# Clearing and first evictions on ScalarE, two-tile norms and a later Q projection in the head of a two-layer attention and MLP kernel

## The chip, the cores and the metric

The kernel runs on one core of a Trainium2 chip. The metric is the device time of one execution in microseconds (us), as the median of several runs. The core has five engines with a queue of instructions each: TensorE (PE in the profile), VectorE (DVE), ScalarE (ACT), GpSimd (POOL) and SyncE (SP, which here only issues DMAs).

## The reference

Two layers run one after the other over the same 2048 tokens of width 512. Each has an attention with 32 query heads of size 16 that share one K and one V, and then a mixer with an MLP:

```python
def _A_ref(x, wq, wk, wv, wo):          # H = 32, Dh = 16
    q = (x @ wq).reshape(B, S, H, Dh).transpose(0, 2, 1, 3)
    k = x @ wk
    v = x @ wv
    p = softmax(einsum("bhqd,bkd->bhqk", q, k) * Dh ** -0.5)
    o = einsum("bhqk,bkd->bhqd", p, v)
    return o.transpose(0, 2, 1, 3).reshape(B, S, H * Dh) @ wo

def _B_ref(x, w1, w2, w3, w4):
    h = gelu(layernorm(x) @ w1)
    hs = concatenate([g0, g1, g2, g3], -1) @ w2   # quarters of h, moved by +1, -1, +2, -2 tokens
    x1 = x + hs
    return x1 + gelu(layernorm(x1) @ w3) @ w4

x = x + _A_ref(layernorm(x), ...);  x = x + _B_ref(layernorm(x), ...)   # layer 0
x = x + _A_ref(layernorm(x), ...);  x = x + _B_ref(layernorm(x), ...)   # layer 1, same weights
```

## The kernel before

**A planner writes the order.** Every piece of work is declared with `op(engine, emit, reads, writes, dur, prio)`. `Plan.run` is a list scheduler: it keeps a modelled clock for each engine and, whenever one is free, takes the ready operation with the lowest `prio` number. The result is a fixed order for each engine, which the hardware then follows in order, with semaphores between engines. A change of one early operation therefore can re-order everything declared later. The length of an operation in the plan is `dur`; `port=True` keeps those GpSimd and VectorE operations apart that share a memory port in the plan.

**Attention.** The 2048 queries of a layer are cut into chunks of 512 (the last two of layer 1 have 256), and each chunk into 8 blocks of 4 heads. A block meets 16 tiles of 128 keys, and each tile in two halves of two heads. In all there are 2048 halves of 128x1024 scores. A half takes one of two ways. In the first, TensorE makes the scores (`qk`, L1011) and ScalarE takes the exponential into `EA` (L1055), with two slots in PSUM so that two halves are under way. In the second, VectorE makes an approximate exponential with integer arithmetic (`J`, L1076), and GpSimd or VectorE add two shifted copies (`JK`, L1086); the program calls such a half a pair. The method `assign` gives a half to the second way when VectorE has time and its inputs are there. TensorE then multiplies with V (L1134): from `VP` for the first way, from `VD`, three scaled copies of V, for the second. The sum of a block is kept in one PSUM bank, `ACC`.

**Layer passage.** In the first chunk of layer 1 the keys of layer 1 are not all there yet. The blocks therefore run over the first 6 tiles of keys, then up to 11, then the rest. At the end of the first two passes VectorE spills `ACC` to memory (L1152) or adds to what was spilled (L1146), fourteen times in all. Meanwhile the MLP of the last chunk of layer 0 is finished and K of layer 1 is made from it (`next_kv`, `ln_in`, `kv`, L868).

**Between scores.** Gelus run on ScalarE (L1385, L1465). They need a table load, and another one before the next exponential. Where TensorE would be idle, `filler` inserts matmuls of zeros (`PB<-ONES,NIL`, L631) to keep it busy.

**The head** (`head`, L665) is what the change touches. `load_x` (L672) fetches x in eight loads of two tiles. GpSimd clears `VD` and `QT` (`fill`, L684), since K and Q lie there in slices with zeros between. Then for each of the four chunks of four tiles: `ln_in` takes statistics (L743), a reciprocal root by GpSimd's power (L763, its input made at L765), the normalised rows (`apply`, L780), and eight or sixteen transposes on TensorE (L798) with VectorE's copies to `YT` (L805). In layer 0 the four tiles of a chunk go through each step together; in layer 1 they go in portions of two, through `across` (L825, L830). `kv` makes K (L868, evicted at L875) and V (L883, evicted at L888 and L893). `qproj` makes Q: with `direct=True` block by block with its zeros (L940, evicted at L947), else in pairs of blocks (L631, evicted to `QS` at L922) which SP's DMAs spread to `QT` (L928).

In the head the lines that set the order of Q are:

```python
        for c in range(4):
            tiles = list(range(4 * c, 4 * c + 4))
            self.ln_in(0, tiles, prio=-6 + 0.5 * c)
            self.kv(0, tiles, prio=-6 + 0.5 * c)
            if c == 0:
                self.qproj(0, 0, prio=-6, blocks=(0, 1), direct=True)
            if c == 2:
                self.qproj(0, 0, prio=-5, blocks=range(2, 8))
```

So blocks 0 and 1 of the first chunk come straight after its K and V, and blocks 2 to 7 after K and V of the third chunk.

Of the kernel before, what the change touches and what calls it, by code (L numbers as in the profile page):

```python
# [485 lines left out]
def t_ps(n):  # L486
    return 0.066 + n * 1.043e-3
# [6 lines left out]
def t_x2(n):  # L494
    return 0.066 + n * 0.522e-3
# [14 lines left out]
class Kernel:  # L510
# [154 lines left out]
    def head(self):  # L665
# [40 lines left out]
        vd = [("VD", i, t) for i in range(2) for t in range(16)]  # L706
        fill("POOL", self.VD, 0.0, vd, 2.8, -7)
        for j in range(3):
            fill("POOL", self.VD[:, j, :, :, 16:17], self.PARTS[j], vd, 0.2, -7)
        fill("POOL", self.QT[:, 0, 2:8, :], 0.0, [("QT", 0, b) for b in range(2, 8)], 2.7, -7)  # L710
        fill("POOL", self.QT[:, 1, :, :], 0.0, [("QT", 1, b) for b in range(8)], 3.6, 2)
        for c in range(4):
            tiles = list(range(4 * c, 4 * c + 4))
            self.ln_in(0, tiles, prio=-6 + 0.5 * c)
            self.kv(0, tiles, prio=-6 + 0.5 * c)
            if c == 0:
                self.qproj(0, 0, prio=-6, blocks=(0, 1), direct=True)
            if c == 2:
                self.qproj(0, 0, prio=-5, blocks=range(2, 8))
        fill("POOL", self.SELC, 0.0, [("SELC",)], 0.1, 3)  # L720
# [91 lines left out]

    def across(self, tiles, dst, dtags, base=None):

        op = self.pl.op
        rows, name = base or (self.ZR, "ZR")
        n = len(tiles)
        L = Late()
        for hd in range(2):
            def fpe(e, hd=hd):  # L820
                ins = None
                for dc in (2 * hd, 2 * hd + 1):
                    for i, tb in enumerate(tiles):
                        x = (dc * n + i) * 128
                        ins = e.transpose(self.PBH[:, L.bank, x:x + 128], rows[:, tb % 4, dc * 128:(dc + 1) * 128],  # L825
                                          self.IDENT)
                return ins
            op("PE", fpe, reads=[(name, tb % 4) for tb in tiles] + [("ID",)], writes=[L], pe=mm(128, 2 * n),
               take=L if hd == 0 else None)
        op("DVE", lambda e: e.tensor_copy(dst, self.shaped(self.PBH[:, L.bank, 0:512 * n], [4, n * 128])),  # L830
           writes=[L] + dtags, dur=t_x2(512 * n), give=L)

    def ln_in(self, la, tiles, prio=None):

        op = self.pl.op
        c = tiles[0] // 4
        src = (lambda tb: self.X16[:, tb, :]) if la == 0 else (lambda tb: self.X32[:, tb, :])
        base = (self.QS, "QS") if la and tiles[0] > 2 else (self.ZR, "ZR")
        slot = (c + la) % 3
        for part in self.portions(tiles) if la else [tiles]:  # L840
            self.stats(src, part, lambda tb: ("X", tb), prio)
            self.rstd(part, prio)
            for tb in part:
                self.apply(base[0][:, tb % 4, :], src(tb), tb, [("X", tb)], [(base[1], tb % 4)],
                           0.456 if la else 0.355, prio)
            n0 = (part[0] % 4) * 128
            dst = self.YT[:, slot, :, n0:n0 + 128 * len(part)]
            if la:
                self.across(part, dst, [("YT", slot, hd, t % 4) for t in part for hd in range(2)], base)
            else:  # L850
                self.transpose(part, dst, [[("YT", slot, hd, t % 4) for t in part] for hd in range(2)], prio, base)

    def yt_tags(self, la, tiles):
        return [("YT", (t // 4 + la) % 3, hd, t % 4) for hd in range(2) for t in tiles]

    def kv(self, la, tiles, prio=None):
        op = self.pl.op
        slot = (tiles[0] // 4 + la) % 3
        n0 = (tiles[0] % 4) * 128
# [3 lines left out]
        for h in range(2):  # L863
            def fpe(e, h=h):
                ins = None
                for dc in (2 * h, 2 * h + 1):
                    for g in range(4):
                        ins = e.matmul(self.PB[32 * g:32 * g + 32, L.bank, 0:n], lhsT=self.WK[:, dc, :],  # L868
                                       rhs=self.YT[:, slot, dc, n0:n0 + n], start=(dc == 0), stop=(dc == 3),
                                       tile_position=(0, 32 * g), skip_group_check=True)  # L870
                return ins
            op("PE", fpe, reads=rd + [("WK",)], writes=[L], pe=("P",) + mm(n, 2)[1:] + (range(4),), prio=prio,
               take=L if h == 0 else None)
        k0 = tiles[0] * 128
        op("DVE", lambda e: e.tensor_copy(self.KT[:, la, k0:k0 + n], self.PB[:, L.bank, 0:n]),  # L875
           writes=[L] + [("KT", la, t) for t in tiles], dur=t_ps(n), prio=prio, give=L)
        M = Late()

        def fv(e):
            ins = None  # L880
            for i, tb in enumerate(tiles):
                for dc in range(4):
                    ins = e.matmul(self.PB[:, M.bank, 32 * i:32 * i + 32],  # L883
                                   lhsT=self.YT[:, slot, dc, n0 + i * 128:n0 + (i + 1) * 128],
                                   rhs=self.WV[:, dc, :], start=(dc == 0), stop=(dc == 3))
            return ins
# [11 lines left out]

    def qproj(self, la, c, prio=None, blocks=range(8), direct=False, part=None):
        op = self.pl.op  # L900
# [5 lines left out]
        tiles = self.tiles_of(la, c)  # L906
        slot = (tiles[0] // 4 + la) % 3
        n0 = (tiles[0] % 4) * 128
        n = self.size(la, c)
        par = self.par(la, c)  # L910
        rd = self.yt_tags(la, tiles)
        for k in () if direct or part == "move" else range(blocks[0] // 2, blocks[-1] // 2 + 1):
            L = Late()
            for h in range(2):
                def fpe(e, h=h, k=k, L=L):
                    ins = None
                    for dc in (2 * h, 2 * h + 1):
                        ins = self.dot(e, L.bank, n, self.WQ[:, dc, 128 * k:128 * k + 128], self.YT[:, slot, dc, n0:n0 + n],
                                       dc == 0, dc == 3)
                    return ins  # L920
                op("PE", fpe, reads=rd + [("WQ",)], writes=[L], pe=tiled(n, 2), prio=prio, take=L if h == 0 else None)
# [10 lines left out]
        for b in blocks if direct else ():  # L932
            L = Late()
            for h in range(2):
                def fpe(e, h=h, b=b, L=L):
                    ins = None
                    for dc in (2 * h, 2 * h + 1):
                        for g in range(4):
                            w0 = 64 * b + 16 * g
                            ins = e.matmul(self.PB[32 * g:32 * g + 32, L.bank, 0:n],  # L940
                                           lhsT=self.WQ[:, dc, w0:w0 + 32], rhs=self.YT[:, slot, dc, n0:n0 + n],
                                           start=(dc == 0), stop=(dc == 3), tile_position=(0, 32 * g),
# [589 lines left out]
```

## Time and profile before

| | |
|---|---|
| median of 5 runs | 1569.65 us (1568.95 to 1571.62) |
| profiled execution, its own time | 1571.36 us |
| its span, first to last instruction | 1569.6 us |
| granted TensorE clock | 0.998 |
| TensorE busy | 1535.0 us (98%) |
| ScalarE busy | 1492.7 us (95%) |
| VectorE busy | 1269.9 us (81%) |
| GpSimd busy | 1121.6 us (71%) |

The span begins with the first instruction that the profiler saw. A group line of the profile gives the source line, the engine, what is written and read, how often, the busy time, the mean length of one instruction (overlapping ones count in full there), and the idle time of the engine just before them with what ended it. A timeline line gives start, length, engine, source line, and in a bracket the idle time before it. Engines overlap, so a busy share says nothing on the time by itself; the chain of waits tells what followed what.

### The profile page before, as it was taken

Reading aid. Unit: us, or ns where it says so; the run is one execution under the profiler, and the core shown is the slowest. Engines: PE = TensorE matmul, PEld = TensorE weight load, DVE = VectorE, ACT = ScalarE, POOL = GpSimd, SP = SyncE. Lnnn points to the kernel's source line nnn. Section 1 sums busy time; section 2 is a strip of 40 time slices with the busy share of each in tenths; the row PEclk is TensorE's granted clock in tenths of the full one; section 3 lists DMA queues with packets and bytes.
Section 4 is the critical chain, followed back from the end, with each engine's and each line's share of the span. In section 5 each row is a group of like instructions: output and inputs, shape, how many; then the busy total and the mean of one; then the engine's idle time right before and its main releaser. Section 6 shows DMA issues by size and latency. Waiting matters only on the chain.

```text
span 1569.6 us, 63240 instructions
## 1 busy us (share of the span) xinstructions
PE 1535.0 (98%) x28553; PEld 655.5 (42%) x28553; DVE 1269.9 (81%) x2226; ACT 1492.7 (95%) x1582; POOL 1121.6 (71%) x1183
## 2 busy tenths in 40 slices
PE   8999999999999999999999999999999999999999
PEld 3433333443333443344333434334333334555565
DVE  8877788778888789887876678888788886988863
ACT  4999999999999999999989989999999999999972
POOL 3688888768787668767765566887687756887741
PEclk9999999999999999999999999999999999999999
DMA  6100100001000001000000000100000000000000
GB/s 213 18 5 5 19 6 6 4 6 19 4 6 6 4 5 20 6 4 2 2 2 2 3 7 11 19 5 4 17 11 6 6 6 16 14 8 6 8 13 23
DMA packets 32142, 21.51 MB, mean 14 GB/s; under 512 B 12672, under 2 KB 31360, under 8 KB 31872
## 3 DMA queue, kind: packets, MB, share of 16 engines
q1 hardware_dynamic: 31872, 17.47, 4.6%
q8 instruction: 223, 3.65, 0.9%
q14 instruction: 47, 0.39, 0.1%
HBM read 7.90 MB, written 2.10 MB: 6 GB/s over the span
## 4 chain that ended last, share of the span: by engine, by line
ACT 64%; PE 32%; DVE 3%; DMA 0%; issue 0%; SPq 0%
ACT EA L1055 61%; PE PB L631 12%; PE PB L1011 10%; PE PB L1134 8%; DVE J L1076 2%; ACT GP L1385 1%; ACT L1055 1%; ACT G L1465 1%; PE PB L825 1%; ACT L1385 1%; DVE JK L1086 0%; PE PB L868 0%; DMA X<-in_A_x_dram 0%; DVE ZR L780 0%; DVE ST L743 0%
## 5 line engine op out<-in xcount | busy, mean ns | idle before, releaser
L1055 ACT ACTIVATE EA<-PB 128x1024 bf16<-128x1024 f32 x1495 | 1382.9, 1092 | 36.3 <-PE PB L1011 30.9
L1086 POOL TENSOR_SCALAR JK<-J 128x1024 uint16<-128x1024 uint16 x923 | 979.2, 1061 | 336.3 <-DVE J L1076 200.1
L1076 DVE TENSOR_SCALAR J<-PB 128x512 uint16<-128x512 f32 x1106 | 715.8, 683 | 141.0 <-PE PB L1011 136.2
L1011 PE MATMUL PB<-QT,KT 32*128 32x512 bf16 (+1 forms) x4608 | 625.1, 360 | 17.7 <-ACT EA L1055 7.3
L1134 PE MATMUL PB<-EA,VP 128*32 128x256 bf16 (+1 forms) x6728 | 388.8, 264 | 4.2 <-DVE ACCF L1168 1.4
L1011 PEld LDWEIGHTS PB<-QT,KT 32*128 32x128 bf16 x4608 | 162.9, 91 | 408.3 <-ACT EA L1055 296.4
L1134 PE MATMUL PB<-JK,VD 128*32 128x256 bf16 (+1 forms) x4976 | 290.6, 265 | 1.8 <-POOL JK L1086 1.0
L1134 PEld LDWEIGHTS PB<-EA,VP 128*32 128x32 bf16 x6728 | 160.1, 95 | 155.8 <-issue 123.1
L631 PE MATMUL PB<-ZT,W 128*32 128x512 bf16 (+2 forms) x2816 | 172.7, 343 | 0.0
L1134 PEld LDWEIGHTS PB<-JK,VD 128*32 128x32 bf16 x4976 | 115.0, 95 | 129.0 <-issue 88.2
L1134 PE MATMUL PB<-J,VD 128*32 128x256 bf16 (+1 forms) x2488 | 157.5, 263 | 1.2 <-DVE J L1076 0.6
L1086 DVE TENSOR_SCALAR JK<-J 128x1024 uint16<-128x1024 uint16 x183 | 133.6, 736 | 12.3 <-PE PB L1134 10.1
L631 PE MATMUL PB<-ONES,NIL 128*32 128x512 bf16 x1472 | 134.0, 390 | 4.8 <-DVE ZR L780 2.3
L631 PE MATMUL PB<-W,G 128*32 128x512 bf16 x1624 | 103.6, 380 | 0.4 <-ACT G L1465 0.3
L1460 DVE CAST G<-PB 128x512 bf16<-128x512 f32 (+2 forms) x126 | 72.2, 581 | 29.4 <-PE PB L631 28.8
L1134 PEld LDWEIGHTS PB<-J,VD 128*32 128x32 bf16 x2488 | 61.4, 95 | 39.5 <-issue 24.8
L631 PEld LDWEIGHTS PB<-ZT,W 128*32 128x32 bf16 x2816 | 64.5, 96 | 30.7 <-issue 19.0
L763 POOL TENSOR_TENSOR SM<-SM,MH 128x2 f32<-128x2 f32 (+2 forms) x65 | 47.3, 728 | 23.3 <-DVE SM L765 18.8
L631 PEld LDWEIGHTS PB<-W,G 128*32 128x32 bf16 x1624 | 41.8, 96 | 35.3 <-issue 10.4
L1197 DVE TENSOR_TENSOR OS<-ACCF,PB 128x512 bf16<-128x512 bf16 (+1 forms) x72 | 44.6, 621 | 12.3 <-PE PB L1191 12.1
L631 PEld LDWEIGHTS PB<-ONES,NIL 128*32 128x32 bf16 x1472 | 37.0, 96 | 31.2 <-issue 7.3
L1465 ACT ACTIVATE G<-G 128x1792 bf16<-128x1792 bf16 x29 | 47.0, 1685 | 0.1
(98 smaller groups left out, 874.6 us busy)
## 6 DMA issues: line engine op xcount, KB each, us to landing
OT<-OS SPq DMA_DIRECT2D x424, 8.0 KB, 1.8
W<-in_B_w_dram SPq DMA_DIRECT2D x2, 1792.0 KB, 14.9
X<-in_A_x_dram SPq DMA_DIRECT2D x8, 256.0 KB, 4.9
QT<-QS SPq DMA_DIRECT2D x32, 64.0 KB, 2.4
out_dram<-OUTB SPq DMA_DIRECT2D x16, 128.0 KB, 1.7
OT<-OS SPq DMA_DIRECT2D x104, 4.0 KB, 1.8
W<-in_B_w_dram SPq DMA_DIRECT2D x2, 512.0 KB, 8.2
WQ<-in_A_wq_dram SPq DMA_DIRECT2D x1, 512.0 KB, 4.5
```

The costliest lines, as they stand in the source:

```text
L631: ins = e.matmul(self.PB[32 * g:32 * g + 32, bank, 0:n], lhsT=lhsT[:, 32 * g:32 * g + 32], rhs=rhs, start=start, stop=stop, tile_position= ...
L763: op("POOL", lambda e: e.tensor_tensor(out=out, in0=src, in1=self.MH[:, 0, a:b], op=ALU.pow), reads=tags + [("MH",)], writes=tg(r), dur=0. ...
L825: ins = e.transpose(self.PBH[:, L.bank, x:x + 128], rows[:, tb % 4, dc * 128:(dc + 1) * 128], self.IDENT)
L1011: ins = e.matmul(self.PB[:, bank, j * n:(j + 1) * n], lhsT=self.KT[32 * h:32 * h + 32, la, (kb + j) * 128:(kb + j + 1) * 128], rhs=self.QT ...
L1055: o = q.feeds = op("ACT", lambda e: e.activation(self.EA[:, ea, :, :], self.PB[:, b0:b0 + 2, :], ACTF.Exp, scale=0.25), writes=bk + [("EA" ...
L1076: o = op("DVE", lambda e, i=i, L=L: e.tensor_scalar(out=J[:, i * 512:(i + 1) * 512], in0=self.PB[:, L.bank, :], scalar1=128 * LOG2E * 0.25 ...
L1086: x = op(eng, lambda e, k=k, r=r: e.tensor_scalar(out=self.JK[:, r, :], in0=J, scalar1=float(self.STEPS[k]), scalar2=1.0, op0=ALU.add, op1 ...
L1134: ins = e.matmul(self.PB[32 * x:32 * x + 32, self.ACC, p * hw:p * hw + hw], lhsT=v[:, la, kb + j, :], rhs=ap[:, i, j * w + u * hw:j * w + ...
L1197: op("DVE", lambda e: e.tensor_tensor(out=osm, in0=acc, in1=self.PB[:, M.bank, 0:n], op=ALU.mult), reads=am, writes=[M] + om, dur=t_ps(n), ...
L1385: op("ACT", lambda e: e.activation(self.GP[:, par, :, 2:2 + n], self.GP[:, par, :, 2:2 + n], ACTF.Gelu_apprx_tanh), reads=gt, writes=gt, d ...
L1460: op("DVE", lambda e, f=f, L=L: e.tensor_copy(self.G2[:, f, 0:n], self.PB[:, L.bank, 0:n]), writes=[L] + [(x, f, i) for x in ("G2", "GE") ...
L1465: op("ACT", lambda e, i=i: e.activation(self.G2[:, :, i * 128:(i + 1) * 128], self.G2[:, :, i * 128:(i + 1) * 128], ACTF.Gelu_apprx_tanh), ...
```

## The change

Three things change in the head, and one in the buffers.

- `VD` and `QT` are cleared by ScalarE (`memzero`) instead of GpSimd.
- `ln_in` of layer 0 also runs in portions of two tiles, with `across` for the transposes. The copy of the first portion and the eviction of the first K are on ScalarE.
- Only block 0 of Q comes first, ahead of K and V of the first chunk. Block 1 and blocks 2 to 7 have `prio=3` and wait until K of tile 7 is evicted.
- The normalised rows of the fourth chunk of layer 0 lie in the first half of `ZT` and not in slot 0 of `YT`, where those of the first chunk lie.

```diff
-        fill("POOL", self.VD, 0.0, vd, 2.8, -7)
+        def clear(ap, n, tags, prio):
+            op("ACT", lambda e: e.memzero(ap), writes=tags, dur=0.1 + n / 2400, prio=prio)
+        clear(self.VD, 3072, vd, -7)
         for j in range(3):
             fill("POOL", self.VD[:, j, :, :, 16:17], self.PARTS[j], vd, 0.2, -7)
-        fill("POOL", self.QT[:, 0, 2:8, :], 0.0, [("QT", 0, b) for b in range(2, 8)], 2.7, -7)
-        fill("POOL", self.QT[:, 1, :, :], 0.0, [("QT", 1, b) for b in range(8)], 3.6, 2)
+        clear(self.QT[:, 0, 2:8, :], 3072, [("QT", 0, b) for b in range(2, 8)], -6.5)
+        clear(self.QT[:, 1, :, :], 4096, [("QT", 1, b) for b in range(8)], -6.4)
         for c in range(4):
             tiles = list(range(4 * c, 4 * c + 4))
             self.ln_in(0, tiles, prio=-6 + 0.5 * c)
+            if c == 0:
+                self.qproj(0, 0, prio=-6, blocks=(0,), direct=True)
             self.kv(0, tiles, prio=-6 + 0.5 * c)
-            if c == 0:
-                self.qproj(0, 0, prio=-6, blocks=(0, 1), direct=True)
-            if c == 2:
-                self.qproj(0, 0, prio=-5, blocks=range(2, 8))
+        self.qproj(0, 0, prio=3, blocks=(1,), direct=True, after=[("KT", 0, 7)])
+        self.qproj(0, 0, prio=3, blocks=range(2, 8), after=[("KT", 0, 7)])
...
-    def across(self, tiles, dst, dtags, base=None):
+    def across(self, tiles, dst, dtags, base=None, prio=None, eng="DVE"):
...
-        op("DVE", lambda e: e.tensor_copy(dst, self.shaped(self.PBH[:, L.bank, 0:512 * n], [4, n * 128])),
-           writes=[L] + dtags, dur=t_x2(512 * n), give=L)
+        src = lambda: self.shaped(self.PBH[:, L.bank, 0:512 * n], [4, n * 128])
+        if eng == "ACT":
+            op("ACT", lambda e: e.copy(dst, src()), writes=[L] + dtags, dur=0.06 + 512 * n / 1200, prio=prio, give=L)
+        else:
+            op("DVE", lambda e: e.tensor_copy(dst, src()), writes=[L] + dtags, dur=t_x2(512 * n), prio=prio, give=L)
...
-        slot = (c + la) % 3
-        for part in self.portions(tiles) if la else [tiles]:
+        slot = self.slot(la, c)
+        for part in self.portions(tiles):
...
-            if la:
-                self.across(part, dst, [("YT", slot, hd, t % 4) for t in part for hd in range(2)], base)
+            if True:
+                self.across(part, dst, [x for t in part for x in self.yt_tag(la, t)], base, prio,
+                            "ACT" if not la and part[0] == 0 else "DVE")
...
+    def slot(self, la, c):
+        return 3 if la == 0 and c == 3 else (c + la) % 3
+
+    def yt(self, slot):
+        return self.ZT[:, 0, :, :] if slot == 3 else self.YT[:, slot, :, :]
...
-        op("DVE", lambda e: e.tensor_copy(self.KT[:, la, k0:k0 + n], self.PB[:, L.bank, 0:n]),
-           writes=[L] + [("KT", la, t) for t in tiles], dur=t_ps(n), prio=prio, give=L)
+        if la == 0 and tiles[0] == 0:
+            op("ACT", lambda e: e.copy(self.KT[:, la, k0:k0 + n], self.PB[:, L.bank, 0:n]),
+               writes=[L] + [("KT", la, t) for t in tiles], dur=0.0505 + n / 1200, prio=prio, give=L)
+        else:
+            op("DVE", lambda e: e.tensor_copy(self.KT[:, la, k0:k0 + n], self.PB[:, L.bank, 0:n]),
+               writes=[L] + [("KT", la, t) for t in tiles], dur=t_ps(n), prio=prio, give=L)
...
-    def qproj(self, la, c, prio=None, blocks=range(8), direct=False, part=None):
+    def qproj(self, la, c, prio=None, blocks=range(8), direct=False, part=None, after=()):
...
-        rd = self.yt_tags(la, tiles)
+        rd = self.yt_tags(la, tiles) + list(after)
```

## The prediction

> **What bounds the kernel now.** I read the page's busy shares first, then its chain, then ScalarE's groups, then the timeline of the head and of ScalarE alone.
>
> ```profile
> PE 1535.0 (98%) x28553; PEld 655.5 (42%) x28553; DVE 1269.9 (81%) x2226; ACT 1492.7 (95%) x1582; POOL 1121.6 (71%) x1183
> ACT 64%; PE 32%; DVE 3%; DMA 0%; issue 0%; SPq 0%
> L1055 ACT ACTIVATE EA<-PB 128x1024 bf16<-128x1024 f32 x1495 | 1382.9, 1092 | 36.3 <-PE PB L1011 30.9
> ```
>
> TensorE's 98% holds filler matmuls that keep it busy, so it is no bound by itself. The chain lies 61% on one line, the exponentials L1055. They pipeline: 1382.9 us for 1495 is **0.925 us each**. So up to the last exponential (1512.1 us) the time is the start of the first one, the number of them, the gelus between, and ScalarE's idle gaps. Afterwards a tail of 57 us runs on TensorE (MLP of the last chunk). The group shows only 36.3 us of idle time. Where is it? First the head:
>
> ```profile
> 6.42 0.75 DVE L765 TENSOR_SCALAR SM<-MV 128x4 f32<-128x4 f32 x1
> 7.25 1.02 POOL L763 TENSOR_TENSOR SM<-SM,MH 128x4 f32<-128x4 f32 x1
> 8.07 1.29 DVE L743 BATCH_NORM_STATS2 ST<-X 128x6 f32<-128x512 bf16 x2 [0.90 <-DMA X<-in_A_x_dram]
> 8.28 3.60 POOL L684 MEMSET QT<- 128x4096 bf16 x1
> 9.27 3.79 DVE L780 TENSOR_SCALAR ZR<-X,MV,SM 128x512 bf16<-128x512 bf16 x4
> 15.63 1.05 PE L868 MATMUL PB<-YT,WK 128*32 128x512 bf16 x16
> 19.32 0.68 DVE L947 CAST QT<-PB 128x512 bf16<-128x512 f32 x1
> 19.75 1.94 ACT L1055 ACTIVATE EA<-PB 128x1024 bf16<-128x1024 f32 x2 [17.75 <-PE PB L1011]
> ```
>
> The columns are start, duration, engine, line. The first exponential starts at 19.75 us. The four normalisations L780 take 3.79 us; the groups give 0.375 us as the shortest and 2.80 us as the longest, and the long one ends with GpSimd's memset. Now ScalarE alone, where it idles later:
>
> ```profile
> 418.81 3.77 ACT L1055 ACTIVATE EA<-PB 128x1024 bf16<-128x1024 f32 x4 [0.20 <-PE PB L1011]
> 423.12 1.94 ACT L1055 ACTIVATE EA<-PB 128x1024 bf16<-128x1024 f32 x2 [0.54 <-PE PB L1011]
> 426.58 15.94 ACT L1055 ACTIVATE EA<-PB 128x1024 bf16<-128x1024 f32 x17 [1.52 <-PE PB L1011]
> 816.57 1.94 ACT L1055 ACTIVATE EA<-PB 128x1024 bf16<-128x1024 f32 x2 [4.20 <-PE PB L1134]
> 819.94 26.18 ACT L1055 ACTIVATE EA<-PB 128x1024 bf16<-128x1024 f32 x28 [1.44 <-PE PB L1011]
> 908.72 126.95 ACT L1055 ACTIVATE EA<-PB 128x1024 bf16<-128x1024 f32 x138 [4.75 <-PE PB L1011]
> ```
>
> The bracket is the idle time before a row. From 19.75 to 44 us there are gaps of 3.2 us in all. From 60 to 1513 us there are 15.3 us, and 10.4 of them are the last three rows: the passage from layer 0 to layer 1. So any change moves the time by four terms: first start, count, gaps, tail.
>
> **What the Trainium skill says.** "SBUF — State Buffer", section "Who interferes with whom": VectorE's two-port modes and GpSimd share a port pair under an exclusive lock held for the whole instruction, while ScalarE has its own ports. The trace agrees: the 2.80 us normalisation under the memset against 0.375 us. "ScalarE: Activation LUTs", section "What ACT_TABLE_LOAD costs": a load is 1283 ns, and an ACTIVATE with immediate operands costs 186 ns + 0.833 ns per element. The trace agrees: loads 1283 ns; 1792 elements 1685 ns (priced 1679). "Perfetto Trace Analysis", section on the GPSIMD instruction: GpSimd spans are unreliable. So the 0.737 us that the trace shows for a two-tile power (L763) is uncertain by some tenths.
>
> **The change, part by part**, in the order in which the built program of the changed kernel issues its instructions.
>
> *Clears on ScalarE.* VD and QT become three ACTIVATEs of 1536, 1536 and 2048 elements (four-byte words). By the price: 1.47 + 1.47 + 1.89, less overlap, 4.7 us. ScalarE was idle there (17.75 us). The table load that stood before the first exponential is now before the clears (0.72 to 2.0 us), with no second one, so they end at 6.7 us, before ScalarE's first eviction. Cost nothing, covered by that idle time. GpSimd's 2.66 + 2.76 + 3.60 us of memsets go, and with them the lock. A new wait: GpSimd's strips in VD come after ScalarE's first clear (3.5 us) and the powers queue behind them; the first is needed at 6.3 us, so nothing.
>
> *Two-tile norms.* The first statistics still wait for X until 3.56 us (the loads' queue is untouched). Four at 0.66 us pace; the rstd input for tiles 0 and 1 is ready at 6.25 us instead of 7.17 for all four. Power for 0,1: 6.3 to 7.04; for 2,3: to 7.8. The applies run at 0.37 us: end 8.55 us if the second power does not block the first apply, 9.25 if it does, against 13.06. Then three statistics of tiles 4 to 6 stand ahead of VectorE's copy of the second transpose (2.0 us; X for them landed by 8.07 to 9.7), the copy ends 11.2 to 11.9. ScalarE copies the first transpose beside that (128x1024, about 0.93 us as an exponential), hidden.
>
> *Q first, one block, K by ScalarE.* TensorE: Q block 0, K, each 0.86 us pace: K done 13.1; ScalarE's 128x512 copy about 0.5 us (its 128x384 ones pace at 0.40); VectorE's cast of Q ends 13.6, earlier. Behind ScalarE's two copies only exponentials are queued, which need them. QK at about 13.9, **first exponential 14.3 to 15.0, I take 14.7: −5.0 us**.
>
> *Later Q blocks and VectorE's queue.* Q blocks 1 to 7 go behind the norms of tiles 4 to 15. Block 1 is first needed after 32 halves: 14.7 + 32 × 0.925 = 44 us; its cast comes at about 28. The DMAs that spread Q (L928, now waiting behind later casts on SP, nothing else is queued there) need to land by about 65 us. Hidden. What counts is K: after eight exponentials tiles 4 to 7 are needed. Counting VectorE's order at trace durations, their K cast ends near 22.4 us; with TensorE in order (K, V and a transpose ahead of units 6 and 7) ScalarE waits about 0.4 + 1.6 us there, and K of tiles 8 to 11 (29 us) and 12 to 15 (36 us) are ahead of need (31 and 38 us). With small ones as now, 3.5 us for 3.2: **+0.3 us** (−1.5 to +2.5). The own slot ZT of the fourth chunk removes a wait on Q of chunk 0, off the path.
>
> *Count.* A greedy planner re-plans everything behind the head. The program has 1498 exponentials and 550 VectorE pairs (1495 and 553): **+2.8 us**.
>
> *Gaps at the layer passage.* In the old program the three waits can be read in TensorE's order: 32 fillers between two score matmuls where VectorE's spill copy (L1152) stood behind two normalisations, and 36 fillers around the last transposes and K of layer 1. In the new program no such cluster stands there; the last K is interleaved with scores and 24 fillers lie in that stretch instead of 44. One cluster of 16 fillers and a K remains elsewhere, up to 1 us. So 10.4 goes to about 1.4: **−9 us**, bounds −12 (most of the 15.3) and +6 (one more wait of the 816 us kind, which order alone would not show).
>
> *Tail.* After the last scores 16 W3 matmuls and 8 transposes more, one JK product (8) less: 16 × 0.054 + 8 × 0.069 − 8 × 0.028 = 1.2 us; TensorE had 1 us of fillers and waits there (1512 to 1515 us). **+0.9** (0 to 2).
>
> Sum: −5.0 + 0.3 + 2.8 − 9 + 0.9 = **−10.0 us**. The profiled execution took 1571.36 us (span 1569.6 and 1.76 around it), so it becomes 1561.4; the median of the runs, 1569.65, stands 1.7 below it: 1559.6.
>
> **Rivals.** *Head only*: the layer passage finds waits of the old size at other places, as real delays differ from planned ones (the 2.3 us near 420 us is not visible in the order). Then −1.0: 1568.6. For it: the head's 5 us are half paid back by three exponentials. Against: the large waits of now are all visible in the order. *Slower*: VectorE is in order, and a spill copy behind two applies, one under a GpSimd power or JK, costs 4.20 + 1.44 = 5.6 us. There are fourteen such copies in the passage. If the new order meets one more of these events than the old, it is −1.0 + 5.6: 1574.3; it decides once the gaps after 60 us exceed 15.3 + 4.1 us. *The clears don't free the port*: powers lock as memsets did, each apply of tiles 0 to 3 behind one, 0.7 to 1.5 us: 1561, inside the forecast.
>
> **How the numbers follow.** Forecast 0.72 (own range 1553.5 to 1566), head only 0.18, slower 0.10. A measurement of this kernel can tell about 0.2%, 3.1 us. The forecast's range is all faster; of head only 0.03 is faster and 0.15 the same; of the slower case 0.01 ends within the bound: faster 0.75, same 0.16, slower 0.09. The range takes in head only: 1553.5 to 1569.
>
> **What would show it.** Right: GpSimd without memsets of 128x3072; four applies at 0.4 us; first exponential before 15.2 us; 1498 exponentials at 0.925 us; ScalarE's gaps after 60 us near 6 us, none of 4 us at the layer passage. Wrong: a first exponential after 16 us, or gaps after 60 us still at 15.

## The result and the profile after

The changed kernel takes **1566.26 us** (median of 20 runs, 1566.08 to 1567.77) against 1569.89 us of the kernel before beside it (38 runs): a ratio of **0.9975** (the two medians alone give 0.9977), 95% interval 0.9969 to 0.9981. It is 3.6 us faster at the medians where 10 were forecast. The profiled execution took 1566.21 us, with a span of 1564.4 us.

The page shows ScalarE's groups and the chain much as forecast: 1498 exponentials, now L1076.

```profile
ACT 71%; PE 26%; DVE 1%; POOL 0%; issue 0%; DMA 0%
L1076 ACT ACTIVATE EA<-PB 128x1024 bf16<-128x1024 f32 x1498 | 1384.9, 1089 | 16.3 <-PE PB L1155 9.7
```

The chain lies 68% on L1076 where it lay 61% on L1055, so still less leads past ScalarE than before. Of the 16.3 us of idle time, 9.7 end with products with V (L1155) rather than with scores: in those waits, what ScalarE lacked was a free EA buffer. Before, 30.9 of 36.3 us ended with scores and 4.5 with products with V, 4.20 of these at 816 us. So waits for a buffer have more than doubled, and it matters below.

The head, by its timeline (start, length, engine, line):

```profile
6.33 1.52 POOL L766 TENSOR_TENSOR SM<-SM,MH 128x2 f32<-128x2 f32 x2 [1.93 <-DVE MV L748]
7.08 1.54 DVE L783 TENSOR_SCALAR ZR<-X,MV,SM 128x512 bf16<-128x512 bf16 x4 [0.48 <-POOL SM L766]
8.86 1.01 ACT L835 COPY YT<-PB 128x1024 bf16<-128x1024 bf16 x1 [2.18 <-PE PB L828]
11.35 1.04 PE L961 MATMUL PB<-YT,WQ 128*32 128x512 bf16 x16
12.21 1.04 PE L885 MATMUL PB<-YT,WK 128*32 128x512 bf16 x16
13.30 0.58 ACT L893 CAST KT<-PB 128x512 bf16<-128x512 f32 x1 [3.43 <-PE PB L885]
14.44 1.02 ACT L1076 ACTIVATE EA<-PB 128x1024 bf16<-128x1024 f32 x1 [0.55 <-PE PB L1032]
```

Four normalisations take 1.54 us where they took 3.79, Q precedes K, ScalarE evicts K, and the first exponential starts at 14.44 us instead of 19.75. The head did what was forecast. The layer passage did not. ScalarE's timeline after 60 us has these rows with the larger idle times in the bracket:

```profile
564.39 69.07 ACT L1076 ACTIVATE EA<-PB 128x1024 bf16<-128x1024 f32 x75 [1.73 <-PE PB L1032]
753.82 47.11 ACT L1076 ACTIVATE EA<-PB 128x1024 bf16<-128x1024 f32 x51 [3.15 <-PE PB L1155]
822.08 23.13 ACT L1076 ACTIVATE EA<-PB 128x1024 bf16<-128x1024 f32 x25 [1.85 <-PE PB L1155]
870.60 7.51 ACT L1076 ACTIVATE EA<-PB 128x1024 bf16<-128x1024 f32 x8 [3.81 <-PE PB L1155]
879.01 1.02 ACT L1076 ACTIVATE EA<-PB 128x1024 bf16<-128x1024 f32 x1 [0.91 <-PE PB L1155]
```

The three waits of before (816, 820, 908 us) are gone, and 11.45 us of others stand here, at other places. ScalarE's ledger is the span cut at the first and the last exponential; its parts add up to the span exactly. "Other" is gelus and table loads between the two; idle time counts every gap, small ones too.

| | first exp. | exps | other | idle to 60 us | idle after | tail | span |
|---|---|---|---|---|---|---|---|
| before | 19.75 | 1382.9 | 90.2 | 3.2 | 16.0 | 57.5 | 1569.6 |
| after | 14.44 | 1384.9 | 90.2 | 2.1 | 14.3 | 58.4 | 1564.4 |
| difference | -5.3 | +2.0 | 0 | -1.1 | -1.7 | +0.9 | -5.2 |

The idle column of before holds one thing that is not a wait in the order. The granted clock is the share of full speed that TensorE was given. In this execution of before it was 0.50 from 421 to 426 us, and the two waits that end at 423 and 427 us (2.1 us) fall in that dip; the execution of after had 1.0 throughout. Without them the gaps after 60 us went from 13.9 to 14.3 us, and the differences add up to -3.1 us, close to the medians' -3.6. Of the 53 executions of before taken beside e5, the ten with a mean clock of 1.000 took 1568.8 us in the median, and the 18 of after's 20 with that clock took 1566.2, so with no dip in either the gain is about 2.6 us; whether the old order invites the dip was not tested.

### The profile page after: what moved, and what is told of

Read it like the earlier page. It is cut to its first block, busy times and chain, and to the rows that moved or that the text cites. A ratio compares the mean times of both kernels' runs of the same rounds, so it can differ in the third digit from the quotient of the medians.

```text
span 1564.4 us, 63148 instructions
## 1 busy us (share of the span) xinstructions
PE 1534.2 (98%) x28513; PEld 655.8 (42%) x28513; DVE 1260.2 (81%) x2222; ACT 1501.0 (96%) x1590; POOL 1104.2 (71%) x1178
## 4 chain that ended last, share of the span: by engine, by line
ACT 71%; PE 26%; DVE 1%; POOL 0%; issue 0%; DMA 0%
ACT EA L1076 68%; PE PB L631 11%; PE PB L1032 8%; PE PB L1155 6%; ACT G L1486 1%; ACT GP L1406 1%; ACT L1076 1%; DVE J L1097 1%; ACT L1406 1%; PE PB L828 1%; PE PB L885 0%; DVE ST L746 0%; ACT L1486 0%; PE PB L904 0%; DMA X<-in_A_x_dram 0%
## 5 line engine op out<-in xcount | busy, mean ns | idle before, releaser
L1076 ACT ACTIVATE EA<-PB 128x1024 bf16<-128x1024 f32 x1498 | 1384.9, 1089 | 16.3 <-PE PB L1155 9.7
L1155 PE MATMUL PB<-EA,VP 128*32 128x256 bf16 (+1 forms) x6748 | 385.7, 264 | 1.6 <-DVE ACCF L1189 1.2
L1155 PE MATMUL PB<-JK,VD 128*32 128x256 bf16 (+1 forms) x4936 | 291.7, 265 | 1.4 <-POOL JK L1107 0.8
L1155 PEld LDWEIGHTS PB<-EA,VP 128*32 128x32 bf16 x6748 | 159.4, 95 | 153.2 <-issue 123.1
L631 PE MATMUL PB<-ZT,W 128*32 128x512 bf16 (+2 forms) x2816 | 170.6, 342 | 0.7 <-DVE G L1481 0.2
L1155 PEld LDWEIGHTS PB<-JK,VD 128*32 128x32 bf16 x4936 | 115.3, 95 | 128.8 <-issue 87.7
L1155 PE MATMUL PB<-J,VD 128*32 128x256 bf16 (+1 forms) x2468 | 156.8, 264 | 0.8 <-DVE J L1097 0.4
L631 PE MATMUL PB<-ONES,NIL 128*32 128x512 bf16 x1472 | 133.6, 388 | 2.1 <-DVE J L1097 1.1
L631 PE MATMUL PB<-W,G 128*32 128x512 bf16 x1624 | 103.0, 380 | 0.3 <-ACT G L1486 0.3
L1481 DVE CAST G<-PB 128x512 bf16<-128x512 f32 (+2 forms) x126 | 72.0, 581 | 23.5 <-PE PB L631 22.5
L1155 PEld LDWEIGHTS PB<-J,VD 128*32 128x32 bf16 x2468 | 61.5, 95 | 38.8 <-issue 26.8
L631 PEld LDWEIGHTS PB<-ZT,W 128*32 128x32 bf16 x2816 | 63.6, 96 | 33.5 <-issue 20.2
L766 POOL TENSOR_TENSOR SM<-SM,MH 128x2 f32<-128x2 f32 (+1 forms) x69 | 48.5, 706 | 21.3 <-DVE SM L768 15.0
L631 PEld LDWEIGHTS PB<-W,G 128*32 128x32 bf16 x1624 | 42.0, 96 | 34.7 <-issue 8.8
L631 PEld LDWEIGHTS PB<-ONES,NIL 128*32 128x32 bf16 x1472 | 36.8, 96 | 29.1 <-issue 11.4
```

The lines of the kernel that those rows point to most:

```text
L631: ins = e.matmul(self.PB[32 * g:32 * g + 32, bank, 0:n], lhsT=lhsT[:, 32 * g:32 * g + 32], rhs=rhs, start=start, stop=stop, tile_position= ...
L766: op("POOL", lambda e: e.tensor_tensor(out=out, in0=src, in1=self.MH[:, 0, a:b], op=ALU.pow), reads=tags + [("MH",)], writes=tg(r), dur=0. ...
L1076: o = q.feeds = op("ACT", lambda e: e.activation(self.EA[:, ea, :, :], self.PB[:, b0:b0 + 2, :], ACTF.Exp, scale=0.25), writes=bk + [("EA" ...
L1155: ins = e.matmul(self.PB[32 * x:32 * x + 32, self.ACC, p * hw:p * hw + hw], lhsT=v[:, la, kb + j, :], rhs=ap[:, i, j * w + u * hw:j * w + ...
L1481: op("DVE", lambda e, f=f, L=L: e.tensor_copy(self.G2[:, f, 0:n], self.PB[:, L.bank, 0:n]), writes=[L] + [(x, f, i) for x in ("G2", "GE") ...
```

## Experiments: the start

My theory after the result: a start that is earlier by so much makes the kernel faster by just as much, and the rest is the luck of a new order after the head. Rival: a part of the head's gain is taken back by waits that exist because of it.

**e1, start delayed, order kept.** Four more clears of QT on ScalarE before its first eviction, with a planned length that changes nothing else.

```diff
         clear(self.QT[:, 1, :, :], 4096, [("QT", 1, b) for b in range(8)], -6.4)
+        for _ in range(4):
+            op("ACT", lambda e: e.memzero(self.QT[:, 1, :, :]), writes=[("QT", 1, b) for b in range(8)], dur=-0.15, prio=-6.4)
```

> The changed kernel with four more clears of QT on ScalarE (4 x 1.8 us) between its own clears and its first eviction, which the planner does not see: the order of all other work is the same as in the changed kernel. The first exponential moves from 14.4 to about 19.5 us. If the start of the first exponential carries through to the end (theory), the time is 5 us above the changed kernel, 1571 us, with the same gaps after 60 us (13.7 us). If the passage between the layers waits for something that does not depend on the start (rival: absorbed), it is less than 2 us above, with gaps after 60 us of 10 us or less.

Measured: 1572.18 us, ratio 1.0012 (1.0005 to 1.0018). The first exponential starts 6.05 us later (20.49 us), the time is 5.9 us longer, and the idle time after 60 us is 14.29 us against 14.32. The start carries through in full, and the same order gives the same gaps.

Only 4.0 of the 6.05 us are the delay itself. TensorE stood idle for 3.91 us before the first Q products, and its granted clock was 0.50 from 14 to 20 us, so these took 1.90 us instead of 1.04:

```profile
15.39 1.90 PE L963 MATMUL PB<-YT,WQ 128*32 128x512 bf16 x16 [3.91 <-ACT YT L837]
```

**e2, the clears alone, on the order of before.** ScalarE clears; GpSimd's three memsets stay in the plan but shrink to 16 elements.

```diff
-        fill("POOL", self.QT[:, 1, :, :], 0.0, [("QT", 1, b) for b in range(8)], 3.6, 2)
+        unplanned(self.QT[:, 1, :, :], [("QT", 1, b) for b in range(8)])
+        fill("POOL", self.QT[:, 1, 0, 0:16], 0.0, [("QT", 1, b) for b in range(8)], 3.6, 2)
```

> The kernel before with its clears done by ScalarE without the planner's knowledge; GpSimd's three memsets shrink to 16 elements, so the order of all engines is that of the kernel before. Theory (port lock): the four normalisations fall from 3.79 us to about 1.5 us, the first exponential moves from 19.75 to about 17.4 us, and the time falls by 2.3 us to about 1567.5 us. Rival (the lock costs nothing, X's landing sets the start): 1569.9 us, first exponential unchanged.

Measured: 1567.28 us, ratio 0.9982 (0.9976 to 0.9989). The four normalisations take 1.36 us instead of 3.79, the first exponential starts at 17.57 us, and all later gaps are those of before, the clock dip near 420 us included. Freeing the port is worth 2.2 us of the 5.3 by itself.

## Experiments: the same code, planned again

**e3 and e4, one constant of the planner.** `MARGIN`, the time that the plan allows between another engine and TensorE, goes from 0.150 to 0.151 us, in the changed kernel and in the kernel before. No operation is added or removed by hand.

```diff
-    MARGIN = 0.15
+    MARGIN = 0.151
```

> The changed kernel with one number of the plan's model moved by 1 ns (MARGIN 0.150 to 0.151): the head up to about 170 VectorE instructions is the same, everything behind is planned anew (1493 exponentials instead of 1498). If the order behind the head is worth several us (theory: re-planning), the time differs from 1566.3 by 2 us or more in either direction, with other places of the passage waits. If the time follows from head and count alone (rival): five exponentials less, 4.6 us faster, 1561.7 us, gaps as now.

> The kernel before with MARGIN 0.150 to 0.151: the head is the same, the order differs from about 360 VectorE instructions on, with 1489 exponentials instead of 1495. Theory (re-planning alone is worth several us): 1569.9 plus or minus 2 to 6 us; gaps after 60 us anywhere from 8 to 18 us. Rival (count alone): six exponentials less, 5.5 us faster, 1564.4 us.

Measured: e3 1561.48 us, ratio 0.9945 (0.9932 to 0.9959); e4 1564.75 us, ratio 0.9966 (0.9954 to 0.9979). One nanosecond in the plan of the kernel before brings about what the change did, or a little more (the intervals overlap). Orders differ by several microseconds without any difference in design.

By their sums, these two runs do not speak for the gaps: count alone gave 1561.7 and 1564.4 us, and both came within 0.4 us of it. The exponentials' busy time is 3.4 us less in e3 and 4.4 in e4; the idle time after 60 us is 13.9 and 13.3 us, against 14.3 in the changed kernel and 13.9 in the one before without its dip, at other places. Count and gaps are told apart by e12, e8 and e11.

**e12, a margin of 0.152 us** in the changed kernel gives 1488 exponentials.

> The changed kernel planned with a margin of 0.152 us: 1488 exponentials, the fewest found. Count alone, gaps as in the changed kernel (12.95 us): 1566.3 - 10 x 0.9245 = 1557.0 us. Gaps theory: 1550 to 1559 us by gaps of 6 to 15 us. A candidate for a version that is faster than both.

Measured: 1561.21 us, ratio 0.9945 (0.9928 to 0.9961), above both expectations. The exponentials' busy time is 7.4 us less than in the changed kernel and idle time after 60 us 1.5 less, but the row "other" is 99.2 instead of 90.2 us and the tail 54.0 instead of 58.4: the plan now runs four gelus of 1.69 us, which stood behind the last exponential, between two exponentials, with a pair of table loads (2 x 1.283 us). The count is not a price by itself: a plan with fewer exponentials can pay elsewhere.

## Experiments: parts of the change undone

Each takes one part back and lets the planner run again. Theory then: time = first start + gaps of the head + 0.9245 us per exponential + 164.8 us, the rest being constant. Rival: the parts add.

- e5: the clears back on GpSimd (the three `fill("POOL", ...)` of before).
- e6: `for part in self.portions(tiles) if la else [tiles]` again, with `transpose` for layer 0.
- e7: the Q blocks of the first chunk in the order of before.
- e8: `eng="DVE"` for the first copy to YT, and K of the first chunk evicted on VectorE:

```diff
-                            "ACT" if not la and part[0] == 0 else "DVE")
+                            "DVE")
...
-        if la == 0 and tiles[0] == 0:
+        if False:
```

> The changed kernel with the clears of VD and QT back on GpSimd (all else of the change kept; the plan comes out with 1495 exponentials). Count and start: the time is the start of the first exponential + the gaps of the head + 0.9245 us x exponentials + 164.8 us. The first exponential should start later than 14.44 us, at 17 to 18.5 us, because the memsets lock VectorE's port under the applies again; with head gaps of 2 us that is 17.5 + 2.1 + 1382.1 + 164.8 = 1566.5 us: no slower than the changed kernel, although its head loses 3 us, since three exponentials fewer pay it back. Rival (each part of the change is worth what it moves at the head, the rest stays): 1566.3 + 3.1 = 1569.4 us.

> The changed kernel with layer 0's norms in four-tile steps again (with them the first transpose is evicted by VectorE; clears, K on ScalarE and the Q order stay; the plan has 1490 exponentials). Count and start: first exponential at about 16.3 us (statistics of all four tiles, then one power), 16.3 + 2.1 + 1377.5 + 164.8 = 1560.7 us: faster than the changed kernel by 5 us although its head is slower by 2. Rival (parts add): 1566.3 + 1.9 = 1568.2 us.

> The changed kernel with the order of the Q blocks of the first chunk as before (two blocks ahead of nothing but after K, six after the third chunk's K; 1492 exponentials). Count and start: first exponential about 15.3 us, head gaps 2 to 3.2 us, 15.3 + 2.6 + 1379.4 + 164.8 = 1562.1 us. Rival (parts add): 1566.3 + 0.9 = 1567.2 us, and more if the six later blocks now stand in the way of K.

> The changed kernel with the first K and the first transposes evicted by VectorE (1496 exponentials). Count and start: first exponential about 15 us, 15.0 + 2.1 + 1383.1 + 164.8 = 1565.0 us. Rival (parts add): 1566.3 + 0.6 = 1566.9 us. The two lie close; the start of the first exponential is what this run shows.

| | us | ratio (95%) | first exp. | exps | other | idle to 60 | idle after | tail |
|---|---|---|---|---|---|---|---|---|
| after | 1566.26 | 0.9975 (0.9969 to 0.9981) | 14.44 | 1384.9 | 90.2 | 2.1 | 14.3 | 58.4 |
| e5 | 1571.92 | 1.0012 (1.0005 to 1.0019) | 21.05 | 1384.6 | 90.2 | 2.6 | 13.8 | 57.3 |
| e6 | 1567.10 | 0.9982 (0.9974 to 0.9989) | 16.13 | 1377.4 | 94.4 | 3.3 | 16.9 | 57.3 |
| e7 | 1567.68 | 0.9987 (0.9980 to 0.9994) | 16.35 | 1381.1 | 90.2 | 4.6 | 14.3 | 60.8 |
| e8 | 1558.76 | 0.9930 (0.9914 to 0.9947) | 14.99 | 1383.4 | 90.2 | 2.5 | 7.2 | 58.5 |

My formula failed in all four: it gave 1566.5, 1560.7, 1562.1 and 1565.0 us. Its "constant" holds the gaps, the gelus ahead of the last exponential, and the tail, and these moved. The rival was near for e6 (1568.2) and e7 (1567.2), but 2.5 us too low for e5 (1569.4) and 8.1 too high for e8 (1566.9). Every part did bring the start forward: undoing one costs 6.6, 1.7, 1.9 and 0.6 us of it.

In e5 a memset of 3.51 us, now behind the powers, stood over the first two normalisations (3.60 us for the two). TensorE then stood idle for 2.80 us and had a granted clock of 0.50 from 12 to 18 us, as in e1. Both make the start later than the 17 to 18.5 us expected, and later than before's. The profiled executions of e6 and e7 had dips to 0.50 as well, from 998 to 1001 and from 605 to 608 us, and their waits of 2.77 and 2.76 us end just there (1002 and 609 us): a part of their "idle after" is the clock's.

**e8 is the run that matters.** Its head is the changed kernel's to 1 us, with two exponentials fewer. It is 7.5 us faster, and 7.1 of that are idle time after 60 us. In its ScalarE timeline the waits at 564, 754 and 822 us are not there:

```profile
724.75 66.78 ACT L1076 ACTIVATE EA<-PB 128x1024 bf16<-128x1024 f32 x72
796.06 41.62 ACT L1076 ACTIVATE EA<-PB 128x1024 bf16<-128x1024 f32 x45
863.07 7.51 ACT L1076 ACTIVATE EA<-PB 128x1024 bf16<-128x1024 f32 x8 [3.81 <-PE PB L1155]
```

So here the gaps are the term that decides, and they belong to the order. Against before, e8's idle time after 60 us is down from 16.0 to 7.2 us, or by 6.7 us without the clock dip, where the forecast wanted 9. Two gaps are left as they were, 3.81 us, now at 863, and 0.91 at 871 us.

**e11, e8 planned with a margin of 0.151 us.**

> The version with the first K and transposes evicted by VectorE (e8), planned with a margin of 0.151 instead of 0.150 us: 1492 exponentials instead of 1496, the head's code the same. Count alone, gaps as in e8 (6.0 us): 1558.8 - 4 x 0.9245 = 1555.1 us. Gaps theory (a re-planning draws the gaps anew, from 6 to 15 us in the kernels so far): up to 9 us slower than that, 1555 to 1564 us, with the difference to 1555.1 found in ScalarE's gaps after 60 us.

Measured: 1562.42 us, ratio 0.9957 (0.9942 to 0.9972): 3.7 us slower than e8 with four exponentials fewer. Idle time after 60 us is 13.2 us against 7.2, in an execution that took 1564.17 us and had a dip to 0.50 from 1421 to 1423 us, with 1.14 us of waits beside it; the greater part of the 6 us is the order's. As in e12, gelus came out of the tail (52.2 us) with two table loads more.

## Experiments: what makes the gaps

In the changed kernel, the trace around 753.8 us shows this. The last product of a block is done (L1155, JK); VectorE's copy of `ACC` (L1189) stands behind a normalisation (L783); TensorE does 24 products of the MLP; then come the next block's 12 products with EA, which free buffers for ScalarE.

```profile
750.78 0.28 PE L1155 MATMUL PB<-JK,VD 128*32 128x256 bf16 x4
750.88 1.37 DVE L783 TENSOR_SCALAR QS<-X,MV,SM 128x512 bf16<-128x512 f32 x1 [0.82 <-POOL SM L766]
751.53 1.48 PE L631 MATMUL PB<-W,G 128*32 128x512 bf16 x24
752.17 0.67 DVE L1189 CAST ACCF<-PB 128x512 bf16<-128x512 f32 x1
753.47 0.51 PE L1155 MATMUL PB<-EA,VP 128*32 128x256 bf16 x12
```

**e9, shorter normalisations.** Layer 1's input normalisations work on 64 of 512 columns; the rest of each tile is left out.

```diff
-                self.apply(base[0][:, tb % 4, :], src(tb), tb, ...
+                w = 512 if la == 0 else 64
+                self.apply(base[0][:, tb % 4, 0:w], src(tb)[:, 0:w], tb, ...
```

> The changed kernel with its own order of instructions kept, in which layer 1's input normalisations (QS from X, one per tile) work on 64 of 512 columns; the rest of the normalised tile is left out. VectorE theory: VectorE works in order, and the gaps of 3.15 us (753.8) and 3.81 us (870.6) contain a normalisation of 1.37 and 1.10 us that stands ahead of the copy of ACC or the spill that TensorE waits for. At about 0.15 us each they become about 1 us shorter each, so the gaps after 60 us fall from 12.95 to 10.5 to 11.5 us and the time from 1566.3 to about 1564.5 us (1563 to 1565.5). Rival (TensorE's own order, the 24 fillers and the last transposes, set these gaps): gaps unchanged, 1566.3 us.

Measured: 1566.11 us, ratio 0.9977 (0.9969 to 0.9985), and every gap of the passage as it was (3.15, 1.85, 3.81, 0.91 us). But the edit bit less than planned:

```profile
752.11 1.14 DVE L783 TENSOR_SCALAR QS<-X,MV,SM 128x64 bf16<-128x64 f32 x1 [0.81 <-POOL SM L766]
752.16 2.17 POOL L1108 TENSOR_SCALAR JK<-J 128x1024 uint16<-128x1024 uint16 x2
```

An eighth of the columns took 1.14 us instead of 1.37, where the median of these short normalisations is 0.32 us: most of it is the wait for GpSimd, which fits the port lock that the Trainium skill describes in "SBUF — State Buffer", section "Who interferes with whom". At 754 us the run doesn't decide on VectorE; e16 does. At 870 us it says more: the normalisation ahead of the spill took 0.88 us instead of 1.10, but the spill started no earlier in the order, since it waited 0.31 us for the block's last products on TensorE. (The gap at 564 us was 2.94 instead of 1.73 us in this execution, with a granted clock of 0.50 from 562 to 564 us.)

**e16 and e15, the order edited at that one place.** In e16 VectorE's copy goes ahead of the normalisation. In e15, besides, TensorE's 12 products with EA and 8 of J and JK go ahead of 16 of the 24 MLP products. Nothing else moves on any engine.

```diff
+        ahead("DVE", [at("DVE", 746.63)], at("DVE", 745.15))
+        ahead("PE", [at("PE", t) for t in (747.56, 747.67, 747.78, 747.88, 747.99)], at("PE", 746.10))
```

(The numbers are the plan's own start times, by which the edit finds the operations; e16 has the first line only.)

> The same with VectorE's copy moved alone and TensorE's order left as it was. If VectorE's late copy makes the gap, it becomes about 1.9 us; if TensorE's 24 W,G products do, it stays at 3.15 us.

> The changed kernel with its order edited at one place, before the gap of 3.15 us at 753.8: VectorE's copy of the accumulator (L1189) goes ahead of the normalisation (L783) that stood before it, and TensorE's next 12 EA products with 8 of J and JK go ahead of 16 of the 24 W,G products. If the turnover's order makes this gap, the products start at about 752.05 instead of 753.47 us and the gap is 1.7 instead of 3.15 us, all others as they were: the time 1564.9 us (1565.9 if TensorE's order gives most of it back). Rival (a missing buffer or a late GpSimd product holds it): 3.15 us as before.

Measured: e16 1566.3 us (one run). The copy now starts at 751.11, 1.06 us earlier, the products with EA start at 753.47 as before, and the gap stays:

```profile
751.11 0.69 DVE L1206 CAST ACCF<-PB 128x512 bf16<-128x512 f32 x1 [1.05 <-PE PB L1172]
753.81 1.02 ACT L1093 ACTIVATE EA<-PB 128x1024 bf16<-128x1024 f32 x1 [3.15 <-PE PB L1172]
```

TensorE, not VectorE, set this gap. e15: 1566.43 us, ratio 0.9975 (0.9966 to 0.9984). The gap shrinks as expected, but the time does not, since its other half appears 3 us later:

```profile
752.06 0.50 PE L1173 MATMUL PB<-EA,VP 128*32 128x256 bf16 x12
752.39 1.94 ACT L1094 ACTIVATE EA<-PB 128x1024 bf16<-128x1024 f32 x2 [1.64 <-PE PB L1173]
755.83 1.02 ACT L1094 ACTIVATE EA<-PB 128x1024 bf16<-128x1024 f32 x1 [1.50 <-PE PB L1050]
```

1.64 + 1.50 = 3.14 us: the 16 MLP products that were pushed back now delay the scores.

**e13, one buffer more.** Eight EA buffers instead of seven for the first 1456 exponentials, with every engine's order as planned for seven.

```diff
-        self.EA = sb("EA", [self.N_EA, 2, 512])
+        self.EA = sb("EA", [8, 2, 512])
...
+        at = k % 8 if k < 1456 else ea
```

> The changed kernel with eight EA buffers instead of seven for its first 1456 exponentials, planned as with seven, so that every engine's order is that of the changed kernel: exponential k waits for the products of k-8 instead of k-7. If the gaps that end with PE L1155 (3.15, 1.85, 3.81, 0.91) are ScalarE waiting for a free EA buffer while TensorE turns over the accumulator, each becomes shorter by one exponential: about 2.2, 0.9, 2.9, 0 us, 3.7 us in all, and the time 1562.6 us; if TensorE's fixed order gives most of it back (e10 kept 28%), 1565.2 us with new gaps by PE L1032 behind the shortened ones. Rival (scores, not buffers, are what it waits for there): gaps unchanged, 1566.3 us.

Measured: 1565.70 us, ratio 0.9972 (0.9962 to 0.9983). The gaps by products with EA shrink by 0.92 us each, to 2.23, 0.93 and 2.89, and the one of 0.91 is gone, as expected; but a wait for scores of 0.7 us follows each of the three, and only 0.6 of the 3.7 us reach the time:

```profile
753.78 1.02 ACT L1083 ACTIVATE EA<-PB 128x1024 bf16<-128x1024 f32 x1 [2.23 <-PE PB L1164]
755.48 4.77 ACT L1083 ACTIVATE EA<-PB 128x1024 bf16<-128x1024 f32 x5 [0.68 <-PE PB L1038]
```

So ScalarE does wait for a buffer there, but a buffer is not what is missing. What is? The next views are TensorE's busy time in the stretch before a gap, once of all its matmuls and once of the filler matmuls (`NIL`) alone. Columns: stretch, its length, busy time, instructions, granted clock, DMA. First the changed kernel, all and then fillers:

```profile
740.00:755.00 15.00, 15.00 (x253) 1.00 0.01 2
866.00:871.00 5.00, 5.00 (x144) 1.00 0.00 0
```

```profile
740.00:755.00 15.00, 0.00 (x0) 1.00 0.01 2
866.00:871.00 5.00, 0.00 (x0) 1.00 0.00 0
```

The kernel before at its gaps, all and then fillers:

```profile
805.00:820.00 15.00, 13.77 (x210) 1.00 0.01 2
900.00:909.00 9.00, 8.83 (x150) 1.00 0.01 2
```

```profile
805.00:820.00 15.00, 5.11 (x68) 1.00 0.01 2
900.00:909.00 9.00, 4.07 (x48) 1.00 0.01 2
```

These are two kinds of gap. Before, TensorE ran fillers for a good part of the stretch (5.1 of 15 us, 4.1 of 9): both engines waited for a chain through others. At 754 and 870 us after, TensorE is full of real work (15.00 of 15.00 us, no filler): the order has put MLP work where scores were due, and ScalarE runs dry whichever instruction of TensorE it happens to wait for. At 754 us, moving one of them moved the gap. The chain of waits agrees for both places: from 746 to 753.8 us and from 860 to 872 us it runs on TensorE alone, with more than half of it on products of the MLP (L631). (A full TensorE is not enough for a gap: before was full without a filler from 866 to 871 us too, as was e8 from 725 to 750 us, 25.00 of 25.00, and neither has a gap of ScalarE there.)

The other two larger gaps of the changed kernel are not of this second kind. At 564 us TensorE ran 16 fillers between transposes and K of layer 1, a gap of the first kind. At 822 us the chain passes through VectorE's eviction of an MLP product (L1481), for which TensorE's next 16 MLP products waited:

```profile
562.72 0.87 PE L631 MATMUL PB<-ONES,NIL 128*32 128x512 bf16 x12
563.52 0.51 PE L885 MATMUL PB<-YT,WK 128*32 128x384 bf16 x8
821.09 0.83 PE L631 MATMUL PB<-ZT,W 128*32 128x384 bf16 x16 [0.23 <-DVE G L1481]
```

**e10, shorter exponentials.** 25 of the 1498, every 60th, work on 512 of 1024 columns; half of each is left out.

> The changed kernel with its own order kept, in which 25 of the 1498 exponentials, evenly spread (every 60th), work on 512 of 1024 columns; half of those 25 exponentials is left out. This prices the count. If ScalarE bounds the stretch between head and tail everywhere, 25 x 0.427 us = 10.7 us go: 1555.6 us. Rival (TensorE and VectorE follow close behind, and each exponential saved comes back as a gap): gaps after 60 us grow, and 1561 us or more remain.

Measured: 1563.24 us, ratio 0.9959 (0.9945 to 0.9974): 3.0 us less than the changed kernel and not 10.7. The exponentials' busy time fell by 6.9 us only (a short one among long ones saved 0.28 us each, not the 0.427 that 512 columns cost at the 0.833 ns of the prediction's price), and idle time after 60 us grew by 3.6: about half comes back as waits on a fixed order, as the rival said.

**e14, e8 with eight EA buffers** in the same way.

> The version with the first K and transposes evicted by VectorE (e8), its order kept, with eight EA buffers in the same way. Its gaps by PE L1155 are 3.81 and 0.91 us: 1.8 us less, 1557.0 us; a candidate for the fastest version. Rival (given back by TensorE's order): 1558.3 us.

Measured: 1558.05 us, ratio **0.9925** (0.9910 to 0.9940). At the medians it is the fastest version here, 8.2 us below the changed kernel. Of that, 7.5 are e8's order; the eighth buffer's 0.7 lie within the intervals, near the rival's 1558.3.

## Why the prediction was wrong, step by step

- **Start, -5.0 forecast, -5.31 measured.** Right in its steps: the powers ran at 6.33, the second did not hold up the first normalisation, Q and K followed each other at 0.86 us, ScalarE's copy of K took 0.58 us, and e1 shows that the whole start arrives in the time. The clears ran from 2.02 to 6.68 us, 4.66 us where the price of the Trainium skill, "ScalarE: Activation LUTs", section "What ACT_TABLE_LOAD costs", had given an estimate of 4.7.
- **Head gaps, +0.3 forecast, -1.1 measured.** Mis-sized: K of tiles 4 to 7 was expected to cost 2.0 us of waits; the gaps there were 0.90 and 0.26 us.
- **Count, +2.8 forecast, +2.0 measured; tail, +0.9 forecast, +0.9 measured.** Sizes as said, though e10 and e12 show that the count is no price that carries to another order. (The 2.8 was 3 x 0.925; the busy time of all exponentials rose by 2.0.)
- **Gaps after 60 us, -9 forecast, -1.7 measured, and +0.4 without the clock dip of before: the step that failed.** It read, in TensorE's order, that the three large waits of before go with clusters of fillers, and that "in the new program no such cluster stands there" but one of 16 with a K, "up to 1 us". That reading was right: the three waits are gone, and the one cluster fits the gap at 564 us (1.73 us). The conclusion, that some 10.4 us become 1.4, was not: fillers show only the gaps in which TensorE has nothing to do. The new order's gaps at 754 and 870 us (3.15 and 3.81 us) stand where TensorE has no filler at all and is full, and e15 and e16 show its order to be what holds ScalarE at 754. The reasoning had no term for waits of this kind, nor for those at 822 and 879 us. Besides, 2.1 us of the old waits were the clock dip, which the text took for a wait that the order doesn't show.
- **The rival "head only"** said what happened (waits of the old size at other places) and came nearer, 1568.6 us, with too small a gain from the head gaps and the count. Its reason, that "real delays differ from planned ones", is not what the runs show: the gaps recur at 3.15, 1.85, 3.81 and 0.91 us in e1, e9, e10 and e16. A delay that the plan gets wrong every time would recur as well, but around 754 us the plan's own start times (745.15, 746.63 and 747.56 us for the normalisation, the copy and the products with EA) lie 5.5 to 5.9 us before the measured ones, so on these three the plan's times fit the chip's within 0.4 us. The chance of 0.18 for this rival was too small, since the argument against it was the step that failed.
- **The rival "slower"**, a copy of `ACC` behind normalisations, did occur at 750.9 us; e16 shows that it cost nothing there.

What stays open: which property of e8's plan keeps it free of the gaps at 564, 754 and 822 us (the 3.81 us before 871 it keeps). The order was edited at 754 us alone; that 870 us has the same cause is read from TensorE's full stretch and the chain, and no run tested the gaps at 564 and 822 us.

## What to carry to other kernels

When a planner orders everything behind an edit, forecast the edit's own place and give the re-ordering a range of its own: here a nanosecond in one planning constant moved the time by 5 us, where the change moved it by 3.6. In such an order, look for gaps of the bounding engine in both kinds of stretch: where the feeding engine has only fillers, and where it has none and is full; a wait that ends with a buffer coming free may be neither the buffer's nor the copy's. And test a suspected wait by moving it while the order is kept, then look for its other half a few microseconds later.

## What the runs showed of the hardware

- A normalisation that met a GpSimd operation took 1.14 us for 64 columns, where 512 columns took 1.37 us at the same place of the order; the GpSimd operations beside it take about 1.04 us each. Moved to 751.72 us in e16, 512 columns took 0.54 us, so the time depended on where it met them more than on its size.
- When TensorE had stood idle for 3.91 us (e1) and 2.80 us (e5) in the head, its granted clock fell to 0.50 and came back only at 20 and 18 us; after 2.32 us idle in the head of the kernel before it stayed at 1.00. The same dip to 0.50, for 3 to 7 us, lies once or twice in the profiled executions of before, e2, e3, e6, e7, e9, e11 and e12, with a wait of ScalarE in it or at its end.
- With one order, ScalarE's gaps repeat to 0.02 us from run to run and under a shift of 6 us (e1), so a gap that is bigger in one execution points to the clock: the wait at 564 us was 1.73 us, and 2.94 in the profiled execution of e9, with its dip at that place.
